# LayerNorm statistics of x rows 4 to 7 moved to ScalarE, the filter's constant term in 32-column quarters, four PSUM buffers for part of the products, 22 warm-up matmuls, new instruction orders

## The chip, the cores and the metric

One core of one Trainium2 chip. The time is device time of one execution in microseconds (us); the profile gives one execution in detail. Engines: TensorE (PE, its weight loads PEld), VectorE (DVE), ScalarE (ACT), GpSimd (POOL), and SyncE (SP), which issues most of the DMAs.

## The reference, cut to what matters

The kernel computes the output and the nine gradients of one transformer-like block. `mod` is silu(c) times a weight matrix, cut into six rows; part A is a spectral filter, part B a two-layer MLP with squared ReLU. x has 2048 rows of 512 in bf16, the MLP is 1792 wide.

```python
mod = (silu(c) @ w_mod).reshape(6, -1)
sa, ca, ga, sb, cb, gb = mod
h = layernorm(x) * (1 + ca) + sa
x = x + ga * irfft2(rfft2(h) * (w_r + 1j * w_i))
h = layernorm(x) * (1 + cb) + sb
r = max(einsum('bsd,df->bsf', h, w1) + b1, 0)
x = x + gb * (einsum('bsf,fd->bsd', r * r, w2) + b2)
```

Returned are x and, for a given gradient of it, the gradients of all inputs.

## The kernel before, in words

x is held as 16 row tiles of 128 rows by 512 columns (t = 0 to 15; "rows 4 to 7" are tiles of that numbering). The Fourier transforms are matmuls with cosine and sine tables that the kernel computes itself. The MLP's width is cut into 14 chunks of 128 columns, the 2048 rows into 4 blocks of 512 (b = 0 to 3).

The work around the change, in the order of the code:

- **Start.** A loop of 30 matmuls of a constant (L759 and L760, operand ones_sq) writes the two PSUM buffers mm_0s and mm_1s of pool mmps; nothing reads the results. silu(c) is spread over 128 columns by four ACT copies (L768) into scb, a part of the tile that the profile calls gab. `build_ta` (L124 to L128) makes a sine table. SP loads x in four pieces of 512 KB (L727), w2 in three (L735), w_mod in pieces (L724), the first block of the output's gradient (L742).
- **mod.** `mod_rows(1)` multiplies w_mod with scb (L784) and ACT writes 1 + ca to modb (L785). `mod_rows(2, 5, 4, 3)` computes four rows at once in 32-column strips of the array (L789).
- **Turned operands.** `turn_w2` turns w2 by TensorE (L814), and DVE or ACT (L817, L819) writes it to w2T, through PSUM pool psW with two buffers; `turn_g0` does the same for the first gradient block (L825; DVE L827, ACT L829) into gT_0s.
- **LayerNorm and first transform.** `row_stats` takes two row tiles: one bn_stats each (L837) and bn_aggr (L838) on DVE, then the reciprocal standard deviation and nb, minus the mean times it (L842). `row_norm` normalises (L847), stores (L849), multiplies by modb (L851), folds (`fold1`, L277 and L278); then four matmuls for each row tile (L313, L314) and an ACT eviction (L315) write utcs.
- **Products.** `back_products(b)`: for each chunk four matmuls of 512 columns (L912, w2T by gT) into a buffer of mmps, evicted into gab by DVE (L914, every fifth chunk) or ACT (L916). The products of blocks 0 to 2 are spread by the order table between the other work.
- **The constant term.** sa, the constant that LayerNorm's output gets, is transformed separately: 16 matmuls of 128 columns (L891), one DVE eviction (L892) to dcrow, and two matmuls (L350) with the 0/1 mask ind add it into the first second-stage tile psB.
- **Second stage.** `spec_f23`: matmuls into psB (L355), one ACT eviction to AE (L359), third-stage matmuls into psC (L338), ACT eviction (L339). ACT also makes tables lf_w for it from integer phases (L250).
- **Later.** The MLP forward and backward (L1086 to L1121, L1095 adds up a bias gradient), the weight gradients (L1389), the filter's backward pass, in which a helper copies PSUM to gmbc (ACT, L490), multiplies it four times on DVE (L500), and complex products p are made on DVE (L444, L445).

The order on every engine is not that of the code: the table `ORDER` (from L505) lists for PE, DVE, ACT, POOL and SP the numbers of all their instructions, and `set_order` chains each engine's instructions in that order. An engine executes its list strictly one after the other.

Of the kernel before, what the change touches and what calls it, by code (L numbers as in the profile page):

```python
# [9 lines left out]
AF = mybir.ActivationFunctionType  # L10
ALU = mybir.AluOpType
# [7 lines left out]
D = 512  # L19
# [305 lines left out]
def spec_f23(tc, K, UT, AEs, dc, dest, elementwise, after=lambda gi: None):  # L325

    nc = tc.nc
    with Slots(tc, name="psB", bufs=1, space=PSUM) as psB_pool, \
# [14 lines left out]
        for gi in range(8):  # L343
            ps = psB_pool.tile([P, 2, 2, 256], FP32, name="psB")
            for hh in range(2):
                for b in (1, 0):
                    extra = dc is not None and gi == 0 and hh == 0 and b == 0
                    if extra:
                        for cs in range(2):
                            nc.tensor.matmul(ps[64 * cs:64 * cs + 64, hh, b, :], lhsT=dc[0], rhs=dc[1][:, 256 * cs:256 * cs + 256], start=True, stop=False,  # L350
                                             tile_position=(0, 64 * cs))
                    for e in range(2):
                        for cs in range(2):
                            c = 2 * e + cs
                            nc.tensor.matmul(ps[64 * cs:64 * cs + 64, hh, b, P * e:P * e + P], lhsT=UT[:, c, 2 * (2 * gi + hh) + b, :, :],  # L355
                                             rhs=K["Cd"][:, P * c:P * c + P], start=not extra, stop=(e == 1 if extra else True), tile_position=(0, 64 * cs))
# [113 lines left out]
class GMod:  # L470
# [12 lines left out]
    def emit(self, jc, q, row, pool, ppool, nbuf=2, last=False):  # L483
# [147 lines left out]
def kernel(  # L631
# [286 lines left out]
    for b in range(NB - 1):  # L918
        back_products(b)
# [744 lines left out]
```

## Time and profile before

| | |
|---|---|
| median of 3 runs | 390.41 us (390.37 to 390.8) |
| profiled execution | 391.62 us |
| its span (first to last instruction) | 389.8 us, so 1.82 us lie around it |
| PE busy | 376.9 us, 97% |
| DVE busy | 336.1 us, 86% |
| ACT busy | 303.9 us, 78% |
| POOL busy | 35.1 us, 9% |
| granted TensorE clock, mean of the span | 1.00 |

How to read it: busy time is an average over stages that differ. The stages used here are cut at events that the trace shows: the first product (14.80 us), the first psB matmul (46.86), the first psG matmul of the transform back (70.51), and the end of that transform near 99.75. A timeline row gives start and duration in us, engine, source line, operation, out<-in, shape, count, and in brackets how long the engine stood idle before and which instruction released it.

### The profile page before, as it was taken

Reading aid. Unit: us, or ns where it says so; the run is one execution under the profiler, and the core shown is the slowest. Engines: PE = TensorE matmul, PEld = TensorE weight load, DVE = VectorE, ACT = ScalarE, POOL = GpSimd, SP = SyncE. Lnnn points to the kernel's source line nnn. Section 1 sums busy time; section 2 is a strip of 40 time slices with the busy share of each in tenths; the row PEclk is TensorE's granted clock in tenths of the full one; section 3 lists DMA queues with packets and bytes.
Section 4 is the critical chain, followed back from the end, with each engine's and each line's share of the span. In section 5 each row is a group of like instructions: output and inputs, shape, how many; then the busy total and the mean of one; then the engine's idle time right before and its main releaser. Section 6 shows DMA issues by size and latency. Waiting matters only on the chain. (4 is left out here: it accounts for less than half of the span.)

```text
span 389.8 us, 8395 instructions
## 1 busy us (share of the span) xinstructions
PE 376.9 (97%) x3027; PEld 205.1 (53%) x3051; DVE 336.1 (86%) x823; ACT 303.9 (78%) x601; POOL 35.1 (9%) x117
## 2 busy tenths in 40 slices
PE   7999999989999999999999999999899999999996
PEld 2565677544444444444444445447678655444455
DVE  5999969959897479999999999992999976989975
ACT  4787999889888489859986998347476458889793
POOL 5652011000000000000000000010022000010111
DMA  8997989954696869559938899999899989999997
GB/s 273 366 250 201 227 157 229 307 177 176 202 241 154 215 163 183 124 122 281 305 77 176 204 265 190 284 266 314 216 273 321 257 216 298 207 288 223 255 297 231
DMA packets 132429, 89.75 MB, mean 230 GB/s; under 512 B 86974, under 2 KB 118212, under 8 KB 132132
## 3 DMA queue, kind: packets, MB, share of 16 engines
q1 hardware_dynamic: 131376, 86.79, 87.5%
q0 software_dynamic: 832, 2.36, 1.7%
q8 instruction: 24, 0.39, 0.4%
q14 instruction: 17, 0.14, 0.1%
q10 hardware_dynamic: 180, 0.07, 0.1%
HBM read 39.23 MB, written 31.36 MB: 181 GB/s over the span
## 5 line engine op out<-in xcount | busy, mean ns | idle before, releaser
L1389 PEld LDWEIGHTS <-h_sb 128*64 128x64 bf16 (+1 forms) x464 | 32.3, 109 | 14.7 <-issue 2.1
L1086 PEld LDWEIGHTS <-w 128*128 128x128 bf16 x224 | 21.3, 98 | 27.0 <-issue 3.0
L1389 PE MATMUL mm_0s<-gab,h_sb 128*64 128x384 bf16 (+2 forms) x288 | 35.0, 345 | 0.2 <-DMA h_sb<-h_dram 0.2
L1095 ACT ACTIVATE gab<-gab 128x512 bf16<-128x512 bf16 x56 | 34.8, 629 | 0.0
L1121 PEld LDWEIGHTS <-gab 128*128 128x128 bf16 x224 | 21.7, 98 | 24.7 <-ACT gab L1095 0.3
L912 PEld LDWEIGHTS <-w2T 128*128 128x128 bf16 (+1 forms) x280 | 24.2, 102 | 18.3 <-issue 3.8
L1488 PEld LDWEIGHTS <-gab 128*128 128x128 bf16 x192 | 18.6, 98 | 17.8 <-issue 1.4
L1121 PE MATMUL og_1s<-w1T,gab 128*128 128x512 bf16 x111 | 26.9, 379 | 0.1
L1121 PE MATMUL og_0s<-w1T,gab 128*128 128x512 bf16 x106 | 26.5, 379 | 0.2
L1389 PE MATMUL mm_1s<-gab,h_sb 128*64 128x512 bf16 (+2 forms) x176 | 23.7, 370 | 1.4 <-ACT gmbc L490 1.4
L1086 PE MATMUL mm_1s<-h2T,w 128*128 128x512 bf16 x84 | 23.2, 379 | 0.8 <-ACT gab L916 0.3
L1086 PE MATMUL mm_0s<-h2T,w 128*128 128x512 bf16 x80 | 21.9, 379 | 0.0
L1488 PE MATMUL mm_1s<-g_sb,gab 128*128 128x512 bf16 (+1 forms) x95 | 19.7, 352 | 0.4 <-DVE g_sb L1510 0.4
L1488 PE MATMUL mm_0s<-g_sb,gab 128*128 128x512 bf16 (+1 forms) x93 | 19.8, 352 | 0.1
L359 ACT ACTIVATE AE<-psB 128x1024 bf16<-128x1024 f32 x16 | 16.6, 1039 | 1.4 <-issue 1.2
L912 PE MATMUL mm_0s<-gT_0s,w2T 128*64 128x512 bf16 (+1 forms) x76 | 16.6, 380 | 0.6 <-DVE gab L914 0.5
L1086 PE MATMUL pst<-h2T,w 128*128 128x512 bf16 x60 | 16.9, 379 | 0.0
L912 PE MATMUL mm_0s<-gT_1s,w2T 128*128 128x512 bf16 (+1 forms) x64 | 16.0, 379 | 0.3
L912 PE MATMUL mm_1s<-gT_1s,w2T 128*128 128x512 bf16 (+1 forms) x68 | 16.1, 379 | 0.2
L912 PE MATMUL mm_1s<-gT_0s,w2T 128*128 128x512 bf16 (+1 forms) x72 | 15.8, 379 | 0.0
L321 POOL MEMSET AE<- 128x4 bf16 x4 | 0.5, 116 | 167.7 <-DVE h_6s L1089 167.7
L916 ACT CAST gab<-mm_1s 128x512 bf16<-128x512 f32 x24 | 14.3, 597 | 1.4 <-PE mm_1s L912 1.2
(619 smaller groups left out, 1045.3 us busy)
## 6 DMA issues: line engine op xcount, KB each, us to landing
w<-in_B_w_dram SPq DMA_DIRECT2D x2, 1792.0 KB, 7.1
Xb<-xs_dram SPq DMA_DIRECT2D x4, 514.0 KB, 6.2
Z<-wz_dram SPq DMA_DIRECT2D x4, 514.0 KB, 6.3
x_sb<-in_A_x_dram SPq DMA_DIRECT2D x4, 512.0 KB, 7.2
n_dram<-x_sb SPq DMA_DIRECT2D x4, 512.0 KB
h_dram<-h2r SPq DMA_DIRECT2D x8, 256.0 KB, 2.8
gx_dram<-n2rows SPq DMA_DIRECT2D x8, 256.0 KB, 5.1
h_sb<-h_dram SPq DMA_DIRECT2D x4, 512.0 KB, 4.7
```

Of the source, the lines that this page charges most:

```text
L321: nc.gpsimd.memset(ae[:, :, :, 256:257], 0.0)
L359: nc.scalar.activation(dst, ps.rearrange("p r b (e f) -> p (r b) f e", e=2), AF.Copy, scale=EF_S)
L912: nc.tensor.matmul(ps[m], lhsT=w2T[:, dc, fc * P + m.start:fc * P + m.stop], rhs=gT[b][:, :, dc, :], start=(dc == 0), stop=(dc == 3), **pos)
L916: nc.scalar.copy(out=gaT[b][:, fc, :], in_=ps)
L1086: nc.tensor.matmul(ps, lhsT=w1[:, dc, (fc + i) * P:(fc + i + 1) * P], rhs=h2T[b][:, :, dc, :], start=(dc == 0), stop=(dc == 3))
L1095: nc.scalar.activation(gh[:, i, :], gh[:, i, :], AF.Copy, accum_out=gb1[:, b, fc + i:fc + i + 1])
L1121: nc.tensor.matmul(ps, lhsT=lhs(fc), rhs=rhs[:, fc, :], start=(fc == 0), stop=(fc == NFC - 1))
L1389: nc.tensor.matmul(blocks(ps[m], fb), lhsT=h2_sb[:, t, dc * P + m.start:dc * P + m.stop], rhs=gh_rows(t, fb), start=(t == 0), stop=(t == N ...
L1488: nc.tensor.matmul(ps[:, 0:w], lhsT=h_rows(fc, t), rhs=g_sb[:, t, c:c + w], start=(t == 0), stop=(t == NT - 1))
```

## The change

Six edits, and new tables for all five engines' orders:

1. Statistics of row tiles 4 to 7 (`row_stats_act`): ACT sums each row tile with a Copy that accumulates, and sums the squared deviations with a Square that accumulates; three small POOL operations and the same reciprocal replace bn_stats and bn_aggr of these four tiles.
2. The constant term in quarters: its four parts lie in four 32-partition strips, so 16 matmuls of a 32-column operand at four places of the array (four side by side) replace 16 of a 128-column one; the eviction has 128 instead of 512 columns, and the two matmuls that add it become four of half the width. The masks are written by POOL instead of DVE.
3. w2's and the gradient's PSUM tiles in psW get the shape of a product's tile, and products 9 to 13 of block 0 and 0 to 9 of block 1 go round over four buffers (two of mmps, two of psW) instead of two.
4. 22 instead of 30 matmuls of the constant at the start.
5. One ACT copy of 512 columns instead of four of 128 for scb.
6. New orders on every engine.

```diff
@@ spec_f23
-                    if extra:
-                        for cs in range(2):
-                            nc.tensor.matmul(ps[64 * cs:64 * cs + 64, hh, b, :], lhsT=dc[0], rhs=dc[1][:, 256 * cs:256 * cs + 256], start=True, stop=False, ...
+                            if extra:
+                                nc.tensor.matmul(ps[64 * cs:64 * cs + 64, hh, b, P * e:P * e + P], lhsT=dc[0][:, c], rhs=dc[1], start=True, stop=False, ...
@@ ORDER (five tables, all numbers new; first line of PE's)
-        "0 2 1 4 3 6 5 8 30 10 7 12 9 14 11 16 13 18 15 31 52 56 53 57-58 17 54 20 55 19 59 32-47 21-25 64-67 60-63 27 26 29 "
+        "1 0 3 5 7 9 22 11 2 4 13 6 8 15 44 10 23 48-51 17 12 24-39 45-47 14 16 18 52-59 19-21 68-74 60 75 61-67 40-43 238-242 "
@@ main
-    nc.vector.memset(ind, 0.0)
-    nc.vector.memset(ind[0:1, :, 0:1], 1.0)
+    nc.gpsimd.memset(ind, 0.0)
+    for k in range(4):
+        nc.gpsimd.memset(ind[32 * k:32 * k + 32, k, :, 0:1], 1.0 / 32)
-    for k in range(30):
+    for k in range(22):
-    for dc in range(4):
-        nc.scalar.activation(scb[:, dc, :], ccolf[:, dc:dc + 1].broadcast_to([P, P]), AF.Copy, scale=sigcol[:, dc:dc + 1])
+    nc.scalar.copy(out=scb, in_=sc[:, :, None].broadcast_to([P, 4, P]))
@@ turn_w2 (turn_g0 likewise)
-        ps = psW.tile([P, 8, P], BF16, name="psW")
+        ps = psW.tile([P, D], FP32, name="psW").bitcast(BF16).rearrange("p (a q) -> p a q", a=8)
@@
+    def row_stats_act(t):
+        dev = p0.tile([P, 2], FP32, name="l1_dev", bufs=4)
+        nm = p0.tile([P, 2], FP32, name="l1_nm", bufs=4)
+        for j in range(2):
+            junk = p0.tile([P, D], BF16, name="l1_junk", bufs=2)
+            nc.scalar.activation(junk, x_sb[:, t + j, :], AF.Copy, accum_out=dev[:, j:j + 1])
+        nc.gpsimd.tensor_scalar(nm, dev, -1.0 / D, None, op0=ALU.mult)
+        for j in range(2):
+            junk = p0.tile([P, D], BF16, name="l1_junk", bufs=2)
+            nc.scalar.activation(junk, x_sb[:, t + j, :], AF.Square, bias=nm[:, j:j + 1], accum_out=dev[:, j:j + 1])
+        i1 = inv1[:, t:t + 2]
+        nc.gpsimd.tensor_scalar(dev, dev, 1.0 / D, None, op0=ALU.mult)
+        rstd(nc, i1, dev, K)
+        nbs[t] = p0.tile([P, 2], FP32, name="l1_nb", bufs=4)
+        nc.gpsimd.tensor_tensor(nbs[t], nm, i1, op=ALU.mult)
+
     def row_stats(t):
+        if t in (4, 6):
+            return row_stats_act(t)
@@
-    for c, neg in enumerate(((), (1, 3), (1, 2), (2, 3))):
-        fs, co = slice(P * c, P * c + P), (0, 2, 1, 3)[c]
-        for i in range(4):
-            k = int(i in neg)
-            nc.tensor.matmul(psd[:, P * co:P * co + P], lhsT=sacol[:, k, i:i + 1].broadcast_to([P, P]), rhs=K["Cd"][:, fs], start=(i == 0), stop=(i == 3))
+    for i in range(4):
+        for k, neg in enumerate(((), (1, 3), (1, 2), (2, 3))):
+            nc.tensor.matmul(psd[32 * k:32 * k + 32, :], lhsT=sacol[:, int(i in neg), i:i + 1].broadcast_to([P, 32]), rhs=K["Cd"][:, P * k:P * k + P],
+                             start=(i == 0), stop=(i == 3), tile_position=(0, 32 * k))
@@ back_products
-    def back_products(b):
+    def back_products(b, wide=()):
         for fc in range(NFC):
-            ps = mmps.tile([P, SB], FP32, name="mm")
+            k = (fc in wide and wide.index(fc)) % 4
+            ps = psW.tile([P, D], FP32, name="psW") if k > 1 else mmps.tile([P, SB], FP32, name="mm")
...
-    for b in range(NB - 1):
-        back_products(b)
+    back_products(0, range(9, NFC))
+    back_products(1, range(10))
+    psW.release()
+    psM.release()
+    psF1.release()
+    back_products(2)
```

**ACT ahead of modb.** ACT's list before the first product, before the change (L785 writes modb, L819 and L829 write the first products' operands w2T and gT_0s):

```order
L768 ACTIVATE gab<-ccolf,sigcol 128x128
L819 ACTIVATE w2T<-psW_0s,gb2x 128x512
L829 COPY gT_0s<-psW_1s 128x1024
L785 ACTIVATE modb<-mod_ps,onef 128x512
L916 CAST gab<-mm_1s 128x512
```

and the same place of the changed kernel (its L839 and L843 are the sums and squared sums, L786 writes modb, L830 gT_0s):

```order
L839 ACTIVATE l_junk_0s,l_dev_1s<-x_sb 128x512
L839 ACTIVATE l_junk_1s,l_dev_1s<-x_sb 128x512
L820 ACTIVATE w2T<-psW_0s,gb2x 128x512
L769 COPY gab<-sacol 128x512
L830 COPY gT_0s<-psW_1s 128x1024
L843 ACTIVATE l_junk_1s,l_dev_1s<-x_sb,l_nm_1s 128x512
L843 ACTIVATE l_junk_0s,l_dev_1s<-x_sb,l_nm_1s 128x512
L786 ACTIVATE modb<-mod_ps,onef 128x512
L820 ACTIVATE w2T<-psW_0s,gb2x 128x640
```

All eight new activations stand ahead of modb, two of them between gT_0s and modb; the other four stand earlier in the list.

**ACT at the first AE.** Before (L359 evicts psB, L250 makes a table):

```order
L178 ACTIVATE Cf<-gen_v_1s,npi 128x512
L916 CAST gab<-mm_0s 128x512
L359 ACTIVATE AE_123<-psB 128x4x256
L250 ACTIVATE lf_w_1s<-lf_v,npi 128x1024
L916 CAST gab<-mm_1s 128x512
L359 ACTIVATE AE_124<-psB 128x4x256
```

and after (L358 evicts psB, L931 a product):

```order
L315 CAST utcs<-psA_0s 128x128x4
L250 ACTIVATE lf_w_1s<-lf_v,npi 128x1024
L358 ACTIVATE AE_123<-psB 128x4x256
L931 CAST gab<-psW_1s 128x512
```

The fourth table L250 has moved from behind the first AE to ahead of it, and products now sit in psW as well.

**DVE in the backward filter.** Before (L500 reads gmbc, L444 and L445 make complex products, all on DVE):

```order
L500 SCALAR_TENSOR_TENSOR gm_junk,gsc<-wmc_0s,onef,gmbc 128x512
L445 TENSOR_TENSOR p_3967<-Xb,G_0s 128x1028
L444 TENSOR_TENSOR p_3966<-Xb,G_0s 128x1028
L500 SCALAR_TENSOR_TENSOR gm_junk,gsc<-wmc_0s,onef,gmbc 128x512
L446 TENSOR_TENSOR Xb<-p_3966 128x2x257
```

and after:

```order
L499 SCALAR_TENSOR_TENSOR gm_junk,gsc<-wmc_0s,onef,gmbc 128x512 x2
L445 TENSOR_TENSOR Z_3880<-p_3956 128x2x257
L444 TENSOR_TENSOR p_3963<-Xb,G_0s 128x1028
L499 SCALAR_TENSOR_TENSOR gm_junk,gsc<-wmc_0s,onef,gmbc 128x512
L443 TENSOR_TENSOR p_3962<-Xb,G_0s 128x1028
```

One product p instead of two stands between the third and the fourth of a group of four multiplications by gmbc.

On SP the third piece of x is now loaded fourth in all, ahead of the gradient's first block and the piece of w_mod that modb needs.

## Rows read from the trace of the kernel before

**Rows 1.** Windows by stage: us, busy PE PEld DVE ACT POOL, PEclk, DMA, GB/s.

```profile
0.00:14.80 14.80, 12.62 (x83) 5.85 (x85) 10.85 (x57) 6.70 (x12) 7.90 (x44) 1.00 0.90 305
14.80:46.90 32.10, 31.34 (x244) 18.42 (x245) 32.10 (x118) 27.81 (x47) 11.33 (x34) 1.00 0.92 246
46.90:70.50 23.60, 23.27 (x324) 17.35 (x323) 19.86 (x51) 23.36 (x39) 2.92 (x8) 1.00 0.97 203
...
250.00:389.80 139.80, 133.48 (x1308) 80.67 (x1313) 116.56 (x269) 97.95 (x185) 12.83 (x30) 1.00 1.02 263
```

**Rows 2.** Timeline of PE from the start to the first product.

```profile
2.54 0.63 PE L760 MATMUL mm_0s<-ones_sq 128*128 128x512 bf16 x1
2.97 0.63 PE L760 MATMUL mm_1s<-ones_sq 128*128 128x512 bf16 x1
...
6.89 0.38 PE L760 MATMUL mm_0s<-ones_sq 128*128 128x512 bf16 x1
...
13.72 1.03 PE L784 MATMUL mod_ps<-wm_0s,gab 128*128 128x512 bf16 x3
...
14.80 1.03 PE L912 MATMUL mm_1s<-gT_0s,w2T 128*128 128x512 bf16 x4
```

**Rows 3.** Timeline of ACT, 4 to 15 us.

```profile
8.43 0.40 ACT L124 ACTIVATE TA<-ta_v,npi 128x128 bf16<-128x128 int32 x1 [1.93 <-DVE ta_v L121]
8.74 0.97 ACT L768 ACTIVATE gab<-ccolf,sigcol 128x128 bf16<-128x128 f32 x3
11.05 0.69 ACT L819 ACTIVATE w2T<-psW_0s,gb2x 128x512 bf16<-128x512 bf16 x1 [1.34 <-DVE gb2x L807]
...
13.59 1.01 ACT L829 COPY gT_0s<-psW_1s 128x1024 bf16<-128x1024 bf16 x1 [0.54 <-PE psW_1s L825]
14.79 0.69 ACT L785 ACTIVATE modb<-mod_ps,onef 128x512 bf16<-128x512 f32 x1 [0.19 <-PE mod_ps L784]
```

**Rows 4.** Timeline of SP's queue, and DMA issues to 20 us with time to landing.

```profile
1.67 0.43 SPq L735 DMA_DIRECT2D gab<-in_B_w_dram  x1
...
gab<-in_B_w_dram SPq DMA_DIRECT2D x1, 512.0 KB, 6.4
```

**Rows 5.** Windows: 10 to 20 us.

```profile
10.00:20.00 10.00, 9.77 (x93) 5.84 (x93) 9.96 (x38) 7.50 (x12) 6.33 (x27) 1.00 1.08 365
```

**Rows 6.** Line L837 on DVE, one buffer: ns min/median/max, first and last start.

```profile
L837 DVE BATCH_NORM_STATS2 l_st_1s<-x_sb x4: 675/680/695, 5.1 to 32.3; 128x6 f32<-128x512 bf16 x4
```

**Rows 7.** Groups of ACT instructions that accumulate: busy us, mean ns.

```profile
L1095 ACT ACTIVATE gab<-gab 128x512 bf16<-128x512 bf16 x56 | 34.8, 629 | 0.0
L1095 ACT ACTIVATION_READ_ACCUMULATOR gab<-gab 128x1 f32 x56 | 11.2, 200 | 0.0
```

**Rows 8.** Timeline of PE: four-strip matmuls, a waiting product, the constant term.

```profile
29.97 0.60 PE L789 MATMUL mod_ps<-wm_1s,gab 128*32 128x512 bf16 x2
...
31.55 0.38 PE L912 MATMUL mm_0s<-gT_0s,w2T 128*128 128x512 bf16 x1 [0.54 <-DVE gab L914]
...
41.48 0.89 PE L891 MATMUL mod_ps<-Cd,sacol 128*128 128x128 bf16 x13
42.20 1.03 PE L912 MATMUL mm_0s<-gT_1s,w2T 128*128 128x512 bf16 x4
```

**Rows 9.** Timeline of DVE: the last fold ahead of the second stage.

```profile
44.61 0.41 DVE L278 TENSOR_TENSOR fold_u_1s<-h_1s 128x512 bf16<-128x512 bf16 x1
```

**Rows 10.** Timeline of ACT: the table behind the first AE.

```profile
48.63 1.14 ACT L250 ACTIVATE lf_w_1s<-lf_v,npi 128x1024 bf16<-128x1024 int16 x1
```

**Rows 11.** Timelines of DVE, ACT and PE around 276 us.

```profile
275.91 0.69 DVE L444 TENSOR_TENSOR p<-Xb,G_0s 128x1028 bf16<-128x1028 bf16 x1
276.51 0.74 DVE L500 SCALAR_TENSOR_TENSOR gm_junk<-wmc_0s,onef,gmbc 128x512 bf16<-128x512 bf16 x1
...
277.37 0.59 ACT L490 CAST gmbc<-mm_1s 128x512 bf16<-128x512 f32 x1 [2.65 <-DVE gm_junk L500]
...
278.01 1.70 PE L1389 MATMUL mm_1s<-gab,h_sb 128*64 128x512 bf16 x14 [1.37 <-ACT gmbc L490]
```

More of the change, by code (lines that the diff above doesn't have):

```diff
@@ L347, in spec_f23 @@
                     extra = dc is not None and gi == 0 and hh == 0 and b == 0
-                    if extra:
-                        for cs in range(2):
-                            nc.tensor.matmul(ps[64 * cs:64 * cs + 64, hh, b, :], lhsT=dc[0], rhs=dc[1][:, 256 * cs:256 * cs + 256], start=True, stop=False,
-                                             tile_position=(0, 64 * cs))
                     for e in range(2):
@@ L354, in spec_f23 @@
                             c = 2 * e + cs
+                            if extra:
+                                nc.tensor.matmul(ps[64 * cs:64 * cs + 64, hh, b, P * e:P * e + P], lhsT=dc[0][:, c], rhs=dc[1], start=True, stop=False,
+                                                 tile_position=(0, 64 * cs))
                             nc.tensor.matmul(ps[64 * cs:64 * cs + 64, hh, b, P * e:P * e + P], lhsT=UT[:, c, 2 * (2 * gi + hh) + b, :, :],
-                                             rhs=K["Cd"][:, P * c:P * c + P], start=not extra, stop=(e == 1 if extra else True), tile_position=(0, 64 * cs))
+                                             rhs=K["Cd"][:, P * c:P * c + P], start=not extra, stop=True, tile_position=(0, 64 * cs))
             ae = AEs[gi % 2]
@@ L681 @@
     AEs = make_ae(nc, lfp)
-    dcrow = lfp.tile([P, D], BF16, name="dcrow")
-    ind = lfp.tile([P, NT, 4], BF16, name="ind")
-    nc.vector.memset(ind, 0.0)
-    nc.vector.memset(ind[0:1, :, 0:1], 1.0)
+    dcrow = lfp.tile([P, P], BF16, name="dcrow")
+    ind = lfp.tile([P, 4, NT, 4], BF16, name="ind")
+    nc.gpsimd.memset(ind, 0.0)
+    for k in range(4):
+        nc.gpsimd.memset(ind[32 * k:32 * k + 32, k, :, 0:1], 1.0 / 32)
     gen = Slots(tc, name="gen", bufs=1, side="right")
@@ L821, in turn_g0 @@
     def turn_g0(h):
-        ps = psW.tile([P, 2, 4, P], BF16, name="psW")
+        ps = psW.tile([P, D], FP32, name="psW").bitcast(BF16).rearrange("p (j c q) -> p j c q", j=2, c=4)
         for j in range(2):
@@ L885 @@
     pm = K["pm"]
-    psd = psM.tile([P, D], FP32, name="mod_ps", bufs=1)
-    for c, neg in enumerate(((), (1, 3), (1, 2), (2, 3))):
-        fs, co = slice(P * c, P * c + P), (0, 2, 1, 3)[c]
-        for i in range(4):
-            k = int(i in neg)
-            nc.tensor.matmul(psd[:, P * co:P * co + P], lhsT=sacol[:, k, i:i + 1].broadcast_to([P, P]), rhs=K["Cd"][:, fs], start=(i == 0), stop=(i == 3))
+    psd = psM.tile([P, D], FP32, name="mod_ps", bufs=1)[:, 0:P]
+    for i in range(4):
+        for k, neg in enumerate(((), (1, 3), (1, 2), (2, 3))):
+            nc.tensor.matmul(psd[32 * k:32 * k + 32, :], lhsT=sacol[:, int(i in neg), i:i + 1].broadcast_to([P, 32]), rhs=K["Cd"][:, P * k:P * k + P],
+                             start=(i == 0), stop=(i == 3), tile_position=(0, 32 * k))
     nc.vector.tensor_scalar(dcrow, psd, 128.0, None, op0=ALU.mult)
@@ L901 @@
         nc.sync.dma_start(LF_dram[q], K["LFall"][:, q])
-    psW.release()
-    psM.release()
-    psF1.release()
-    def back_products(b):
+    def back_products(b, wide=()):
         for fc in range(NFC):
-            ps = mmps.tile([P, SB], FP32, name="mm")
+            k = (fc in wide and wide.index(fc)) % 4
+            ps = psW.tile([P, D], FP32, name="psW") if k > 1 else mmps.tile([P, SB], FP32, name="mm")
             for dc in range(4):
@@ L947, in ew_f @@
                 back_products(NB - 1)
-        spec_f23(tc, K, UT, AEs, (ind.rearrange("p a b -> p (a b)"), dcrow), dest_f, ew_f)
+        spec_f23(tc, K, UT, AEs, (ind.rearrange("p c a b -> p c (a b)"), dcrow), dest_f, ew_f)
     lfp.release()
```

182 rows, old and new, of the table ORDER are left out of this document.

## The prediction

> **What bounds the kernel now.** I read the windows by stage first, to see which engine is full where, and then the timelines at the borders of the stages.
>
> Up to 14.80 us no engine is full: DVE is busy for 10.85 us, ACT for 6.70, and PE's 12.62 are mostly matmuls of the constant [rows 1]. What ends this stage is the first product, which needs w2T and gT_0s; gT_0s comes from the copy at 13.59, which lasts 1.01 us, and the product starts at 14.80 [rows 2, 3]. So the start is set by loads, turned operands and their evictions.
>
> From 14.80 to 46.90 DVE is busy in all of 32.10 us, PE in 31.34 and ACT in 27.81 [rows 1]. The stage ends when the last fold, at 44.61 [rows 9], has gone through its matmuls and ACT's eviction. From 46.90 to 70.50 ACT is busy in 23.36 of 23.60 us and PE in 23.27 [rows 1]. In both stages PE is almost full, because products fill its gaps: the idle time of PE is 0.76 and 0.33 us. That is the ceiling for anything that only relieves DVE or ACT there; more can be had only by taking work from PE. From 250 us on PE is idle for 6.32 us [rows 1], and one wait there stands in the way of a single move of the order: 1.37 us at 278.01, for gmbc [rows 11].
>
> **The change part by part.** The sum is made against the profiled execution, 391.62 us, of which 389.8 are span; the median of the runs is 390.41, which is 1.21 lower, and I carry the sum over to it. A measurement of this kernel can tell about 0.2%, 0.78 us, from no change.
>
> *Eight matmuls of the constant fewer.* At the pace of products, four in 1.03 us of which the last shows 0.38, one takes (1.03 - 0.38) / 3 = 0.216 us, so eight are 1.73 us [rows 2]. They fill time in which PE waits for turned operands. Bounds -1.73 and 0; I take 0, since the first product follows ACT's copy and not the matmul before it.
>
> *Loads.* x's third piece is moved ahead of the gradient and of w_mod. 512 KB at the 365 GB/s of 10 to 20 us [rows 5] are 1.44 us. w2's first piece lands at 1.67 + 6.4 = 8.07 us [rows 4]; two more pieces of 512 KB behind it put the gradient at 10.9 and w_mod's at 12.4 now, and at 12.4 and 13.8 after the change. The matmuls on w_mod's piece start at 13.72 now [rows 2], so about 0.1 is lost; bounds 0 and +1.44. With the eviction behind it I take **+0.15** for the first product.
>
> *Statistics.* Four bn_stats of 0.68 us leave DVE [rows 6], -2.7 us of its work. ACT gets eight activations, each with the read of its accumulator: 0.63 us when the 0.20 of the read overlaps, 0.83 when it doesn't [rows 7], in the middle 0.73, 5.8 us in all (5.0 to 6.6). One copy for scb instead of four gives back about 0.7: three took 0.97, so four 1.29, and a 512-column activation takes 0.59 to 0.69 [rows 3, 11]. The 5.1 us left go ahead of modb. ACT's waits there are 1.93, 1.34, 0.54 and 0.19, together 4.0 [rows 3]. So modb comes about 1.1 us later, and behind it in ACT's list stand w2T's evictions; DVE's first multiplication by modb waits for it, and of the 2.7 us some 1.6 are left. PE's ceiling then cuts it: without more idle time on PE the last fold's earlier end is worth what the next two terms say, and nothing by itself. Bounds: 0, and -0.76 if all of PE's idle time goes.
>
> *Four buffers.* The longest wait of a product is 0.54 us, at 31.55, for DVE to evict mm_0s [rows 8]; a product with two more buffers doesn't wait. **-0.5** (bounds -0.76, 0). Covered is it by DVE's order; a later DVE eviction can bring it back.
>
> *The constant in quarters.* Between 41.48 and 42.20 thirteen matmuls of 128 columns pass, 0.055 each [rows 8], 16 take 0.89. In strips of 32 columns two of the same strip start 0.216 apart while the other strips run beside them (two in 0.60 at 29.97) [rows 8], so four strips cost one: 4 x 0.055 = 0.22. **-0.67**; the other bound is 0, if strips of 128 columns don't overlap. The two matmuls into psB become four of half the columns: 0. The shorter eviction and the masks on POOL free DVE a little, under the same ceiling: 0.
>
> Here a rule speaks against the edit. The row shows four-strip matmuls next to full ones without a wait named before or after them [rows 8]. The Trainium skill, page TensorEngine Tiling (Array Packing), section Key Properties, says that a change of the tiling mode drains TensorE; by it the strips would pay for going in and out of the mode, and if that cost all they save, the sum would be -1.3 and the time 389.1. I stay with the row, which is the same kind of matmul in the same place.
>
> *The table behind the first AE.* The 1.14 us of L250 [rows 10] leave the stage in which ACT is full, and go into one in which it has 4.29 us idle [rows 1]. PE can use no more than its 0.33: **-0.3** (bounds -0.33, 0).
>
> *The late wait.* One product p of 0.60 us (275.91 to 276.51) less stands ahead of the multiplication that frees gmbc [rows 11]; PE's wait of 1.37 falls to about 0.7: **-0.65** (bounds -1.37, 0). Late next would be ACT's copy of 0.59 itself.
>
> *Other orders.* Every engine's list is new. The rest keeps the same stages, so 0, with 1 us on each side.
>
> Sum: 0.15 - 0.5 - 0.67 - 0.3 - 0.65 = -1.97, from 391.62 to 389.65 and from the median to **388.4 us**.
>
> **The rivals.**
>
> *The start pays too.* If the matmuls of the constant now hold up the turned operands in PE's list, eight fewer bring the first product forward by up to 1.73: 388.4 - 1.7 = 386.7. For it: PE is busy in 12.62 of 14.80 us. Against: ACT's copy is what the product follows, and its loads move back. Chance 0.10.
>
> *Nothing of DVE's time is used.* modb comes as late as DVE has been relieved, the strips don't overlap, and only the late wait is shorter, -0.5 to -0.65: about 389.9, within the bound. For it: three engines are nearly full in one stage, and what one gives another takes. Chance 0.18.
>
> *Slower: ScalarE becomes the bound.* At 0.83 us each the activations take 6.6 us, of which 4.3 fit (the 4.0 of the waits and a third of a microsecond at the copies): modb and all behind it come 2.3 us late. From 14.80 to 46.90 ACT then has 27.81 + 1.14 + 2.3 = 31.25 of 32.10 us, as tight as PE is now, and with PE's and DVE's results arriving in between it gets nothing back; the first AE comes 2.3 late: 390.41 + 2.3 - 0.65 = 392.1. It decides once modb's delay passes the 2.7 us that DVE saves less what DVE can do in the meantime, or ACT's idle time in this stage falls below about 1 us. Against: DVE has the normalisation of other rows to do until modb is there. By the rows, two activations of 0.63 to 0.83 replace 0.68 of DVE [rows 6, 7], 1.9 to 2.4 times the engine time per row tile. Chance 0.12. The Trainium skill, ScalarE: Activation LUTs, section Rules for kernel authors, has a rule on this side: simple arithmetic belongs on VectorE, which it gives as up to about three times faster per element in bf16. The rows agree in direction.
>
> *Slower: the clock.* The granted clock is at its lower level first: at 2.54 the matmuls are 0.43 us apart, while at 14.80 they are 0.216 apart, so 1.2 and 2.4 GHz [rows 2]. With fewer matmuls of the constant PE does less ahead of the first product. Of the 12.62 us that PE is busy there [rows 1], the 30 matmuls of the constant, about 12 at the lower level and 18 at the higher in that timeline, take 12 x 0.43 + 18 x 0.216 = 9.0, so needed work is 3.6; if the clock stays low until the first product, that takes up to 3.6 longer: 388.4 + 3.6 = 392.0. Against: 22 remain, and the rise comes before 6.89, where a matmul already shows 0.38 instead of 0.63 [rows 2]. Chance 0.05. The Trainium skill, TensorE: Matmul & The Clock Gate, Part 1, states that the throttled level is the default and that activity lifts it; the trace agrees.
>
> **How the numbers follow.** The forecast has the remaining 0.55, with 387.2 to 389.6 as its own range (the terms at their bounds partly add and partly cancel). Faster: forecast and first rival, 0.65. Same: 0.18. Slower: the two last, 0.17. The range from 385.9 to 391.2 holds the forecast, the start's full gain with some luck in the orders, and all of no change, and leaves out most of the slower cases.
>
> **What would show it.** In the changed profile: first product between 14.5 and 15.3; modb's eviction ending near 16.6; DVE no longer full from 14.8 to 46.9; no product of blocks 0 and 1 waiting for an eviction; the 16 strip matmuls in 0.2 to 0.3 us; first AE about 1 us earlier; PE's wait near 276 us at about 0.7. Wrong it is if the first AE comes later than now, if ACT is full ahead of it, or if new waits of over 1 us stand on PE behind 70 us, where I put the new orders at nothing.

## The result and the profile after

The changed kernel takes 394.44 us (median of 4, 393.78 to 394.82) beside 390.39 for the kernel before on the same chip: 1.0107 times as long, 95% interval 1.0081 to 1.0132. It is slower by 4 us where 388.4 was forecast, and outside the range. A second series on another chip gave 394.92 beside 389.74, ratio 1.0115 (1.0085 to 1.0145). The profiled execution took 394.82 us with a span of 393.1.

The windows by stage of the changed kernel, with the columns of [rows 1], cut at the same events (first product, first psB, first psG, end of that transform, first weight-gradient matmul, a little behind the column sums that follow):

```profile
0.00:14.53 14.53, 12.96 (x75) 5.29 (x77) 9.17 (x48) 9.93 (x21) 7.63 (x41) 1.00 0.88 301
14.53:45.80 31.27, 30.80 (x242) 17.37 (x241) 31.17 (x116) 28.92 (x51) 12.21 (x47) 1.00 1.02 262
45.80:68.95 23.15, 22.81 (x326) 16.52 (x325) 18.79 (x48) 22.88 (x38) 2.95 (x9) 1.00 0.98 221
68.95:96.30 27.35, 26.70 (x324) 14.52 (x325) 20.18 (x45) 25.14 (x49) 0.00 (x0) 1.00 0.87 242
96.30:254.90 158.60, 156.17 (x799) 71.46 (x812) 143.85 (x306) 127.05 (x282) 0.00 (x0) 1.00 0.81 188
254.90:266.00 11.10, 7.97 (x58) 3.07 (x56) 5.17 (x11) 1.66 (x3) 1.30 (x6) 0.69 0.93 275
266.00:393.10 127.10, 120.21 (x1208) 75.97 (x1212) 103.96 (x243) 91.03 (x172) 13.32 (x26) 1.00 0.96 256
```

The three last stages of the kernel before, by the same events:

```profile
99.75:256.70 156.95, 155.19 (x788) 71.16 (x800) 140.27 (x298) 125.73 (x279) 0.12 (x1) 1.00 0.84 201
256.70:262.20 5.50, 5.27 (x58) 2.42 (x56) 5.40 (x11) 2.12 (x5) 0.67 (x3) 1.00 1.12 329
262.20:389.80 127.60, 121.56 (x1215) 74.92 (x1218) 104.50 (x243) 91.85 (x174) 12.17 (x28) 1.00 1.00 261
```

Against [rows 1] each of the first three stages is shorter, by 0.27, 0.83 and 0.45 us, and the fourth too (27.35 instead of 29.25). At 96.3 us the changed kernel is ahead by 3.4. It then loses 1.65 in the MLP, and 5.6 in one stretch: 58 matmuls that took 5.50 us take 11.10, at a mean granted clock of 0.69. That stretch on TensorE:

```profile
254.97 1.05 PE L1408 MATMUL mm_0s<-gab,h_sb 128*64 128x512 bf16 x8
259.16 5.33 PE L1408 MATMUL mm_0s<-gab,h_sb 128*64 128x512 bf16 x24 [3.13 <-DMA h_sb<-h_dram]
```

and SP's queue ahead of it (start, issue time, what is loaded):

```profile
246.50 0.58 SPq L1283 DMA_DIRECT2D h_sb<-h_dram  x1
247.18 1.23 SPq L1090 DMA_TRANSPOSE gab<-gab  x1
248.45 2.30 SPq L1276 DMA_TRANSPOSE hr<-h_6s  x1
250.79 2.23 SPq L1276 DMA_TRANSPOSE hr<-h_2s  x1
253.07 1.07 SPq L1283 DMA_DIRECT2D h_sb<-h_dram  x2
```

The first weight gradient reads h_sb in four quarters of 512 KB. The new order issues two of them only from 253.07 on, behind two transposing loads of hr, which is first read at 333.8, about 80 us later. TensorE is through with the first quarter at 256.0 and waits until 259.16. The kernel before, in the same place:

```profile
253.75 0.87 SPq L1264 DMA_DIRECT2D h_sb<-h_dram  x1
...
256.72 1.92 PE L1389 MATMUL mm_0s<-gab,h_sb 128*64 128x512 bf16 x16
258.87 1.92 PE L1389 MATMUL mm_0s<-gab,h_sb 128*64 128x512 bf16 x16 [0.23 <-DMA h_sb<-h_dram]
```

There too the last quarter was issued late, at 253.75, but TensorE had 16 matmuls to do before it and waited 0.23. In SP's table the four loads are 172 to 175, in the order in which TensorE reads them. Before they stood as 175 173 172 174, now as 172 175 174 173: the last to be issued, at 253.7 in both kernels, was the third to be read and is now the second, wanted after 8 matmuls. And the changed kernel begins the gradient 1.75 us earlier. Of the 2.9 us by which its wait is longer, the rows add up to 1.75 for the earlier start, 0.9 for the order and 0.3 for the later landing (259.16 instead of 258.87).

The granted clock (the third last column) follows, in windows of 1 us:

```profile
257.00:258.00 1.00, 0.00 (x0) 0.00 (x0) 0.97 (x2) 0.00 (x0) 0.00 (x0) 1.00 1.01 344
258.00:259.00 1.00, 0.00 (x0) 0.00 (x0) 1.00 (x3) 0.00 (x0) 0.00 (x0) 0.57 0.93 342
259.00:260.00 1.00, 0.84 (x4) 0.36 (x6) 0.91 (x3) 0.00 (x0) 0.00 (x0) 0.50 1.10 363
...
264.00:265.00 1.00, 1.00 (x12) 0.29 (x12) 0.00 (x0) 0.47 (x1) 0.00 (x0) 0.51 0.03 6
265.00:266.00 1.00, 1.00 (x23) 0.46 (x12) 0.23 (x1) 0.12 (x1) 0.00 (x0) 1.00 1.12 212
```

TensorE has done nothing since 256.0; by 259 the clock is at its lower level, 1.2 GHz (0.50), and it stays there until 265, with TensorE busy from 259.16 on. The Trainium skill, TensorE: Matmul & The Clock Gate, Part 1, calls the throttled level the default that activity lifts; the rows agree, with 1.00 again from 265.

### The profile page after: what moved, and what is told of

It is laid out like the page before. It is cut to its first block, busy times and chain, and to the rows that moved or that the text cites. A ratio compares the mean times of both kernels' runs of the same rounds, so it can differ in the third digit from the quotient of the medians.

```text
span 393.1 us, 8396 instructions
## 1 busy us (share of the span) xinstructions
PE 377.6 (96%) x3021; PEld 204.2 (52%) x3045; DVE 332.3 (85%) x811; ACT 306.6 (78%) x614; POOL 37.4 (10%) x128
## 4 chain that ended last, share of the span: by engine, by line
PE 49%; DVE 20%; DMA 11%; ACT 11%; SPq 5%; issue 3%; DVEq 0%; ACTq 0%
PE og_0s L1140 8%; PE og_1s L1140 7%; PE mm_0s L1408 7%; PE mm_1s L1408 4%; PE mm_0s L1507 4%; PE mm_1s L1507 4%; DMA g_sb<-in_grad_out_dram 3%; SPq L1276 2%; PE mm_0s L1105 2%; PE mm_1s L1105 2%; DMA gab<-in_B_w_dram 2%; PE mm_1s L927 2%; DMA Z<-in_A_w_r_dram 2%; DMA x_1s<-in_A_x_dram 1%; DMA h_sb<-h_dram 1%
## 5 line engine op out<-in xcount | busy, mean ns | idle before, releaser
L1408 PEld LDWEIGHTS <-h_sb 128*64 128x64 bf16 (+1 forms) x464 | 34.7, 112 | 15.8 <-DMA h_sb<-h_dram 3.6
L1408 PE MATMUL mm_0s<-gab,h_sb 128*64 128x384 bf16 (+2 forms) x288 | 36.3, 365 | 3.1 <-DMA h_sb<-h_dram 3.1
L927 PEld LDWEIGHTS <-w2T 128*128 128x128 bf16 (+1 forms) x280 | 23.2, 102 | 17.7 <-issue 2.9
L1140 PE MATMUL og_0s<-w1T,gab 128*128 128x512 bf16 x108 | 27.4, 379 | 0.5 <-ACT gab L1114 0.2
L358 ACT ACTIVATE AE<-psB 128x1024 bf16<-128x1024 f32 x16 | 16.6, 1040 | 3.6 <-PE psB L354 2.8
L400 PEld LDWEIGHTS <-utcs 128*128 128x128 bf16 x128 | 10.3, 98 | 9.1 <-issue 1.5
L927 PE MATMUL mm_1s<-gT_0s,w2T 128*128 128x512 bf16 (+1 forms) x68 | 14.6, 380 | 0.0
L927 PE MATMUL mm_1s<-gT_1s,w2T 128*128 128x512 bf16 (+1 forms) x60 | 14.3, 378 | 0.1
L927 PE MATMUL mm_0s<-gT_0s,w2T 128*64 128x512 bf16 (+1 forms) x72 | 14.2, 379 | 0.0
L927 PE MATMUL mm_0s<-gT_1s,w2T 128*128 128x512 bf16 (+1 forms) x56 | 14.1, 378 | 0.0
## 6 DMA issues: line engine op xcount, KB each, us to landing
h_dram<-h2r SPq DMA_DIRECT2D x8, 256.0 KB, 4.7
gx_dram<-n2rows SPq DMA_DIRECT2D x8, 256.0 KB, 4.9
```

Source lines behind the costliest of these rows:

```text
L358: nc.scalar.activation(dst, ps.rearrange("p r b (e f) -> p (r b) f e", e=2), AF.Copy, scale=EF_S)
L400: nc.tensor.matmul(ps[:, P * i:P * i + P], lhsT=CS[:, i, t].rearrange("p a b -> p (a b)"), rhs=K["Cf"][:, i, :], start=True, stop=True)
L927: nc.tensor.matmul(ps[m], lhsT=w2T[:, dc, fc * P + m.start:fc * P + m.stop], rhs=gT[b][:, :, dc, :], start=(dc == 0), stop=(dc == 3), **pos)
L1140: nc.tensor.matmul(ps, lhsT=lhs(fc), rhs=rhs[:, fc, :], start=(fc == 0), stop=(fc == NFC - 1))
L1408: nc.tensor.matmul(blocks(ps[m], fb), lhsT=h2_sb[:, t, dc * P + m.start:dc * P + m.stop], rhs=gh_rows(t, fb), start=(t == 0), stop=(t == N ...
```

## The experiments

Each run is compared by its ratio to the kernel before on the same chip, since chips differ by more than some of the effects (389.68 to 390.39 us for the kernel before); the 95% interval stands in brackets. 1% is 3.9 us.

**The two loads moved up.** One move in SP's table (174 and 173 are the two quarters, 170 and 161 the transposing loads):

```diff
-"... 166 175 178 170 161 174 173 162 154 ..."
+"... 166 175 178 174 173 170 161-162 154 ..."
```

> The changed kernel with one move in SP's order: the two loads of h2_sb (a quarter each, 512 KB) that are issued at 253.07 and 253.69 us go ahead of the two transposing loads of hr at 248.45 and 250.79. Theory A, the loss is this late load and the clock that falls while TensorE waits for it: the wait of 3.13 us at 259 is gone, the granted clock of the whole run is back at 1.00, the stretch from the first weight-gradient matmul to the column sums takes about 5.5 us instead of 11.1, and the time is about 389 us (388 to 390.5). Theory B, the new late orders are tight in many places and the next wait takes its place, such as the transposes that now come later: 392.5 to 394.5 us.

It took 391.75 us, ratio 1.0052 (1.0028 to 1.0075), with a clock of 0.999. And on another chip:

> The changed kernel with the two h2_sb loads moved up once more, for the same chip: 1.5 us above the kernel before (0.9 to 2.2).

It took 392.96 us, ratio 1.0081 (1.0067 to 1.0094), 3.2 above the kernel before and outside the 0.9 to 2.2 expected. Against the changed kernel's 1.0107 and 1.0115 the move gives back 0.55% and 0.34% (2.1 and 1.3 us): a part, as neither theory had it. The profile of the first of the two shows why. The stretch is nearly cured: the last column sum starts at 260.1 instead of 265.3. The load that is waited for is issued 4.8 us earlier but lands only 2.4 us earlier, so that a short wait is left:

```profile
256.73 2.78 PE L1320 MATMUL mm_0s<-gab,h_sb 128*64 128x512 bf16 x24 [0.76 <-DMA h_sb<-h_dram]
```

And TensorE's next waits come up (engine, tile, line, what ended it: us in total, times, longest):

```profile
PE mm_1s L487 <- POOL sel L1241: 1.1, 1, 1.1
PE mm_1s L1320 <- ACT gmbc L489: 1.0, 1, 1.0
PE psY_1s L410 <- ACT Tsb_1s L402: 1.0, 1, 1.0
...
PE mm_0s L1320 <- DMA h_sb<-h_dram: 0.8, 1, 0.8
PE mm_0s L1419 <- DVE g_sb L1441: 0.5, 1, 0.5
```

The first of them, for a mask that GpSimd writes, was not in the changed kernel's list of waits: there TensorE came 5 us later. Not tried was the smaller edit, an exchange of 175 and 173 alone, which keeps the transposing loads in their place.

**The wait filled.** TensorE's idle time gets work, and the load stays late. The 14 matmuls stand in TensorE's list just ahead of the one that waits; the single one, ahead of the gradient, keeps the two buffers in turn:

```diff
+    fps = mmps.tile([P, 4, P], FP32, name="mm")
+    nc.tensor.matmul(fps, lhsT=K["ones_sq"], rhs=K["ones_sq"][:, None, :].broadcast_to([P, 4, P]), start=True, stop=True)
+    fps = mmps.tile([P, 4, P], FP32, name="mm")
+    for k in range(14):
+        nc.tensor.matmul(fps, lhsT=K["ones_sq"], rhs=K["ones_sq"][:, None, :].broadcast_to([P, 4, P]), start=True, stop=True)
```

> The changed kernel with 14 matmuls of the constant put into TensorE's list just ahead of the matmul that waits for h2_sb (and one more of them ahead of the first weight gradient, to keep the buffers' turn). Only the wait's idle time is filled, the load is as late as before. Theory A, the wait of 3.1 us also makes the granted clock fall, and that costs as much again: the clock stays at 1.00, the stretch from the first weight-gradient matmul to the column sums takes about 8.4 us instead of 11.1 (5.5 of the kernel before plus the wait), and the time is 391.7 us (391 to 392.7). Theory B, the lower clock there costs nothing by itself, since the next loads are late as well: 394 to 395 us.

It took 391.79 us, ratio 1.0060 (1.0041 to 1.0079), with a clock of 1.00: theory A in the clock and in the stretch, and 1.8 us (2.1 against the second series) by the ratios where 2.7 were expected. TensorE in this kernel:

```profile
255.12 1.05 PE L1320 MATMUL mm_0s<-gab,h_sb 128*64 128x512 bf16 x8
256.11 3.20 PE L1348 MATMUL mm_1s<-ones_sq 128*128 128x512 bf16 x14
259.24 2.78 PE L1320 MATMUL mm_0s<-gab,h_sb 128*64 128x512 bf16 x24
```

The load lands at the same time, near 259.2. Behind the wait 24 matmuls take 5.33 us in the changed kernel and 2.78 here, and the last column sum starts at 262.6 instead of 265.3. So in the stretch the clock that fell during the wait costs 2.7 us, nearly as much as the wait; about 2 of them reach the end.

**Seams between the two orders.** Four kernels take one kernel's order for all that starts before a time and the other's for the rest, on all five engines; of each table SP's numbers at the seam stand here.

```diff
 seam 96.3, changed program
-"... 60 71 61 62 125 66 68 69 ..."
+"... 60 71 121 68 62 66 63 69 ..."
 seam 99.7, program before, changed rest
-"... 60 59 62 66 65 63 73 69 ..."
+"... 60 59 99 95 97 65 73 71 ..."
 seam 130, changed program
-"... 120 79 109 70 130 85 110 121 ..."
+"... 120 79 121 67 64 85 70 78 ..."
 seam 237, changed program
-"... 176 123 157 155 177 164 172 159 ..."
+"... 176 123 170 166 164 159 168 175 ..."
```

> The changed kernel, its own orders for all that starts before 237 us, the orders of the kernel before behind. Theory A, ahead of 237 us the changed kernel keeps some 1.75 us of its 3.4, the rest having been lost in the MLP's new orders (158.6 us instead of 156.95), and only the late orders cost: 388.6 us (388.0 to 389.5), 1.6 above the kernel that goes over at 96.3. Theory B, the MLP's new orders cost nothing by themselves: the same as that kernel within 0.5.

It took 388.89 us, ratio 0.9970 (0.9943 to 0.9998): theory A in the time, and the first version that beats the kernel before, though narrowly. (That the kernel with the seam at 96.3 would be 1.6 us faster still did not come true, as shown below.) With the front and the start of the gradient as in the changed kernel, the old order again issues one quarter late, and TensorE has 16 matmuls to do before it:

```profile
252.92 0.43 SPq L1195 DMA_DIRECT2D h_sb<-h_dram  x1
...
254.86 1.92 PE L1320 MATMUL mm_0s<-gab,h_sb 128*64 128x512 bf16 x16
257.05 1.92 PE L1320 MATMUL mm_0s<-gab,h_sb 128*64 128x512 bf16 x16 [0.27 <-DMA h_sb<-h_dram]
```

The repeat:

> The kernel with the changed orders up to 237 us and the old ones behind once more, for its interval on the chip on which the changed kernel runs too. 1.36 us under the kernel before (1.0 to 1.8).

It took 388.70 us, ratio 0.9973 (0.9952 to 0.9995), 1.04 us under the kernel before. The changed kernel ran beside it:

> The changed kernel once more beside the others: 4 us above the kernel before (3.2 to 4.8), granted clock of the profiled run 0.99, the wait for h2_sb 3.1 us (2.5 to 3.7).

It took 394.92 us, ratio 1.0115, with a clock of 0.991; its wait for h_sb was 3.8 us and the time 5.2 above, both a little over the ranges expected. So with the same front the new late orders cost 394.92 - 388.70 = 6.2 us on this chip; from the first runs it is 4.05 + 1.36 = 5.4 us.

> The kernel before with its orders up to 99.7 us and the changed kernel's orders behind. Theory A, gains and losses add: the rest costs 4.05 + 3.4 = 7.4 us, so about 397.8 us (396 to 399), with the wait for h2_sb and a granted clock below 0.8 around 260 us. Theory B, the rest's loss hangs on arriving early there (a load that lands at a time of its own is waited for only by an engine that is ahead): the wait is shorter by what the front is late, 392 to 394.5 us.

It took 396.47 us, ratio 1.0175 (1.0139 to 1.0210), 6.2 over the kernel before, with a wait for h_sb of 3.7 us and the clock at 0.84 from 257.3 to 268.2. That is theory A, at the low end: the old front makes it no better. TensorE reached the gradient at 257.3, 2.4 us later than in the changed kernel, and waited longer still: the two loads are issued from 255.91 on, 2.8 us later, with the rest of SP's list. So the lead alone doesn't make the wait.

> The changed kernel, its own orders for all that starts before 96.3 us (the end of the first filter), and from there on the orders of the kernel before on all five engines. Theory A, the front is worth the 3.4 us by which the changed kernel is ahead there, and the old rest keeps it: 387.0 us (386.3 to 387.9), no wait of over 1 us for h2_sb. Theory B, the 3.4 us are only work moved behind the border or idle time that comes back as waits for the loads of the MLP's weights: 389 to 390.5 us.

It took 391.12 us, ratio 1.0030 (0.9997 to 1.0062): a miss, nearer to theory B. Behind the seam TensorE waits, as its timeline shows,

```profile
99.83 0.38 PE L1017 MATMUL mm_1s<-h2T,w 128*128 128x512 bf16 x1 [1.45 <-DVE h2T L992]
100.43 0.38 PE L1017 MATMUL mm_1s<-h2T,w 128*128 128x512 bf16 x1 [0.22 <-ACT h2T L994]
```

and the lead over the kernel before is down to 0.6 us where the MLP's second layer begins (first matmul at 111.49 against 112.13). Part of the 3.4 us is work put behind the border. The first 13 us of the MLP, before and after:

```profile
99.75:112.10 12.35, 12.00 (x61) 5.49 (x59) 11.40 (x23) 10.57 (x20) 0.00 (x0) 1.00 0.99 267
```

```profile
96.30:109.90 13.60, 13.24 (x66) 6.14 (x66) 13.10 (x29) 11.45 (x23) 0.00 (x0) 1.00 0.91 233
```

TensorE has 66 matmuls there instead of 61 and is busy for 1.24 us more, so 1.2 of the 3.4 was never won; some 2.2 were, and 0.4 more go until 255 (145.00 us instead of 144.60).

> The changed kernel, its own orders for all that starts before 130 us, the orders of the kernel before behind: the seam lies inside the MLP, where both lists are in step. Theory A, the new orders of the MLP cost 1.65 us by themselves (158.6 instead of 156.95) and the old ones don't: 387.4 us (386.8 to 388.2), 1 to 1.5 below the kernel with the seam at 237. Theory B, the lead at 96 us is partly idle time that is paid back in the MLP's first matmuls in whichever order: 388.4 to 389.6.

It took 389.26 us, ratio 0.9998 (0.9966 to 1.0030): theory B. With the old orders the MLP takes 159.5 us from 96.35 to the first weight gradient, no less than with the new ones (158.6).

**The statistics back on VectorE**, in the best kernel (seam at 237):

```diff
-        if t in (4, 6):
-            return row_stats_act(t)
-        mv = p0.tile([P, 2, 2], FP32, name="l1_mv", bufs=4)
+        mv = p0.tile([P, 2, 2], FP32, name="l1_mv", bufs=8)
-            st = p0.tile([P, 6], FP32, name="l1_st", bufs=4)
+            st = p0.tile([P, 6], FP32, name="l1_st", bufs=8)
```

with the four bn_stats early in VectorE's list, ahead of the copy of gT_0s:

> The kernel with the changed orders up to 237 us and the old ones behind, with the statistics of rows 4 to 7 back on VectorE (four bn_stats with their bn_aggr early in its list, two buffers' worth more for the small results, ScalarE's eight activations and six small GpSimd operations gone). Theory A, TensorE is the ceiling there and the move by itself is worth little: the first second-stage matmul within 0.3 us of 45.9, the time 388.9 us within 0.6. Theory B, VectorE's 2.7 us were the bound of the stage: the first second-stage matmul 1 to 2.7 us later, 390 to 391.5 us.

It took 392.49 us, ratio 1.0058 (1.0033 to 1.0083), more than theory B. The first product waits for VectorE's copy of gT_0s and comes at 17.43 instead of 14.6:

```profile
17.43 0.82 PE L837 MATMUL mm_0s<-gT_0s,w2T 128*128 128x512 bf16 x3 [1.59 <-DVE gT_0s L740]
```

From there to psB the stage takes 31.67 us, 0.4 more than with the change, VectorE having done the four bn_stats before. And behind that copy (the same code; 41 to 44 and 51 to 54 are the bn_stats and bn_aggr in VectorE's table, 25 is the copy):

```diff
-"... 27 29 41-44 177 32 ... 64 34 51-54 71 73 25 72 30 ... 36 184 120 37 168 46 ..."
+"... 27 29 177 32 ... 64 34 71 73 25 41-44 72 30 ... 36 184 120 37 51-54 168 46 ..."
```

> As the kernel with the statistics of rows 4 to 7 back on VectorE, but with the four bn_stats behind the copy of gT_0s in VectorE's list, so that the first product is not behind them. Theory A, VectorE is still full from the first product on in the changed orders (busy in 31.17 of 31.27 us), so its 2.7 us of work come back as a later last fold: the first product stays at 14.6 (within 0.3), the first second-stage matmul comes 1 to 2.7 us later than 45.9, the time 389.8 to 391.5 us. Theory B, TensorE was the ceiling: within 0.4 of 45.9 and 388.9 us.

It took 393.57 us, ratio 1.0115 (1.0076 to 1.0155), more than theory A. The first product stays at 14.55; then TensorE waits for VectorE's eviction of a product:

```profile
20.03 1.02 PE L837 MATMUL mm_0s<-gT_0s,w2T 128*128 128x512 bf16 x4 [3.04 <-DVE gab L839]
```

The clock falls with it (0.95 from 14.6 to 46), and psB starts at 50.65, 4.7 us late. Beside the best kernel's 0.9973 the two places cost 0.85% and 1.42% (3.3 and 5.5 us; the medians of the second and of the best kernel, on one chip, are 4.9 apart). Both put the bn_stats ahead of something that TensorE waits for, in lists that were made without them, so this is the price of these two places, and the move by itself may be worth less. A third place in VectorE's list might cost less; that wasn't tried, and neither was the move alone on the kernel before.

**Single edits on the kernel before.** Fewer matmuls of the constant, the eight ahead of the first product taken out:

```diff
-    for k in range(30):
+    for k in range(22):
```

> The kernel before with one edit: 22 instead of 30 matmuls of the constant, the eight nearest to the first product taken out of TensorE's list. Theory A, they only fill time in which TensorE waits for turned operands: the first product within 0.25 us of 14.8, the same time as the kernel before within 0.5 us, clock 1.00 throughout. Theory B, they hold up the turned operands: the first product up to 1.7 us earlier, 388.7 us. Theory C, they keep the clock up: the clock falls ahead of the first product and the time is 1 to 3 us longer.

It took 391.02 us, ratio 1.0025 (0.9997 to 1.0052), with the first product at 14.93 and a clock of 0.999: theory A, as far as the interval tells, and nothing for B or C. And four buffers:

```diff
-    for b in range(NB - 1):
-        back_products(b)
+    back_products(0, range(9, NFC))
+    back_products(1, range(10))
+    psW.release()
+    psM.release()
+    psF1.release()
+    back_products(2)
```

(with the tiles of psW and `back_products` as in the change)

> The kernel before with its own orders and one edit: products 9 to 13 of block 0 and 0 to 9 of block 1 go round over four PSUM buffers instead of two. Theory A, the wait of 0.54 us at 31.55 is gone and the first second-stage matmul comes 0 to 0.6 us earlier; 389.9 us, not to be told from no change. Theory B, the order table was laid for two buffers, and an evicting engine that is full makes the same product wait elsewhere: no change of either.

It took 390.32 us, ratio 1.0010 (0.9992 to 1.0027). The wait of [rows 8] is gone, and the stage is as long as before, as this window from first product to psB shows:

```profile
14.91:46.97 32.06, 31.47 (x243) 18.15 (x242) 32.06 (x118) 27.85 (x47) 11.33 (x34) 1.00 0.95 249
```

VectorE is still busy all the time. Theory B.

**Where the rest of the late loss lies.** The kernel with the two loads moved, with seams at 262.5 and at 326.8:

```diff
 seam 262.5
-"... 180 183 181 185 187 186 218 182 ..."
+"... 180 183 196 185 187 186 188 190 ..."
 seam 326.8
-"... 224 253 245 261 236 251 256 252 ..."
+"... 224 253 252 243 236 255 256 244 ..."
```

> The changed kernel with the two h2_sb loads moved up, its orders for all that starts before 262.5 us (behind the column sums), the orders of the kernel before behind. Theory A, the 2.9 us that still lie between the kernel with the two loads moved and the one with all old orders from 237 us on are lost behind 262.5, in the backward filter and the last weight gradients: 388.8 us (388.2 to 389.6). Theory B, they are lost between 237 and 262.5: 391 to 392.

It took 390.47 us, ratio 1.0024 (1.0001 to 1.0048): between the two theories.

> The same with the seam at 326.8 us, at the first matmul of the last weight gradient. Theory A, the last 60 us hold most of the 2.9 (59.0 us against 57.1 from the first of these matmuls to the last): 389.7 us (389.2 to 390.3). Theory B, the backward filter holds it (a wait of 1.07 us for sel at 262.9, among others): 391 to 392.

It took 392.37 us, ratio 1.0067 (1.0052 to 1.0082). With 392.96 for no seam on this chip, some 0.6 us are lost behind 327, within the noise of the two intervals, and 1.9 between 262.5 and 327. Theory A of the second run falls, and B holds, a little beyond its figure. From the kernel with the seam at 262.5, 0.24% over the kernel before, to the one with the seam at 237, 0.3% under it, it is another 0.5%, or 2 us. But the seam at 262.5 makes a wait of its own, 2.0 us for gmbc (1.0 without a seam), and behind it the clock is at 0.50 again, so that 24 matmuls that take 2.78 us without a seam take 4.47:

```profile
277.01 4.47 PE L1320 MATMUL mm_1s<-gab,h_sb 128*64 128x512 bf16 x24 [2.01 <-ACT gmbc L489]
```

Wait and clock are 2.7 us in their stretch, so the 2 us can be the seam's, and it is not shown that the orders between 237 and 262.5 still cost anything with the two loads moved. What is left of the loss goes with several waits of around 1 us (sel, gmbc, Tsb, g_sb), none of which was taken away alone: that they are its cause is not shown.

## Why the prediction was wrong

*The step that failed* is the last term, "Other orders": "Every engine's list is new. The rest keeps the same stages, so 0, with 1 us on each side." The late orders cost 5.4 to 6.2 us. I compared the stages' order on TensorE and did not follow SP's list behind 100 us, in which two quarters of h_sb had got behind two transposing loads, the one read second as the last. SP's list could be read before any run; one has to ask of every load whether it now stands behind something that is needed later. The load and the clock behind it are the part of the loss that is shown: moving the two loads gave back 1.3 to 2.1 us. Some 3 to 4 us remain against the kernel with old orders from 237 us on (1.0052 and 1.0081 beside 0.9970 and 0.9973), and their cause stays open, beyond the new waits of about 1 us. The prediction did name the sign, waits of over 1 us on TensorE behind 70 us: two came, 3.1 us for h_sb and 1.4 for g_sb.

*The wait's price.* Even a step that had seen the load would have had to count the clock. The wait of 3.13 us cost 5.6 in its stretch, and the filled wait shows that 2.7 of it are the clock. The clock fell in a place where no rival had put it: behind the longest wait. At the start 22 matmuls are as good as 30. There the column of the granted clock reads 1.00, and the spacing of the matmuls shows the lower level, 0.43 us as in the prediction; it lasts until about 9 us in the changed kernel and 6.3 before, and the first product is no later.

*The front, -1.32 without the late wait.* The kernel with the old orders from 237 us on is 1.04 and 1.36 us faster. That the sum fits is luck. The front's lead includes some 0.7 us won in the fourth stage, for which there was no term (1.9, less the 1.24 of work put behind its border), and of the terms three were wrong in size or reason:

- *Four buffers, -0.5*: 0 alone. *Statistics, "nothing by itself"*: putting them back cost 3.3 to 5.5 us in two places of the changed lists. I had taken PE's 0.76 us of idle time for the ceiling and DVE for covered, with DVE busy in 32.10 of 32.10 [rows 1]. In the second of them the lateness of 4.7 us is a wait of 3.0 with the clock behind it. The stage became shorter by 0.83 with the change, and DVE's work in it by 0.93 (31.17 instead of 32.10). That fits VectorE as the bound, then and now (31.17 of 31.27), against what I wrote would show. It is argued and not shown alone, since PE's work in the stage shrank too, by 0.54.
- *The constant in quarters, -0.67.* The 16 matmuls run four side by side, in about 0.2 us, but they cost TensorE more than that, as these rows of the changed kernel show:

```profile
42.99 0.27 PE L313 MATMUL psA_0s<-TA,fold_u_0s 128*128 128x256 bf16 x1
43.10 0.27 PE L314 MATMUL psA_0s<-TA,fold_u_0s 128*128 128x256 bf16 x1
43.30 0.41 PE L908 MATMUL mod_ps<-Cd,sacol 128*32 128x128 bf16 x16
43.65 0.28 PE L313 MATMUL psA_1s<-TA,fold_u_1s 128*128 128x256 bf16 x1
```

At the pace of 0.11 the strips would start at 43.21; they start at 43.30, and the next full matmul at 43.65, about 0.1 us behind the end of their four rounds. So there is a pause of about 0.1 us at either change of form, the strips take 0.44 us instead of 0.89, and the term was worth 0.45 of TensorE's time. The rows before had the same pause without naming a wait: four matmuls of a product from 29.00 on, 0.216 apart, make room for the next at 29.86, and the first strip starts at 29.96. Whether the kernel's time got any of it is not shown, with VectorE as full as it is.

- *First product, +0.15*: 14.53 and 14.82 in two profiles, so -0.27 and 0; eight matmuls fewer, 0: right.
- *modb 1.1 us later*: right, at 0.9. Its eviction starts at 15.70 instead of 14.79, and each activation with its read costs 0.62 (the sums) to 0.71 (the squares), start to start:

```profile
11.07 0.62 ACT L839 ACTIVATE l_junk_0s<-x_sb 128x512 bf16<-128x512 bf16 x1
...
11.69 0.62 ACT L839 ACTIVATE l_junk_1s<-x_sb 128x512 bf16<-128x512 bf16 x1
...
15.00 0.72 ACT L843 ACTIVATE l_junk_0s<-x_sb,l_nm_1s 128x512 bf16<-128x512 bf16 x1
...
15.70 0.68 ACT L786 ACTIVATE modb<-mod_ps,onef 128x512 bf16<-128x512 f32 x1
```

- *The table behind the first AE, -0.3*: the stage is 0.45 shorter, with ACT busy for 22.88 us instead of 23.36; the move was not run alone.
- *The late wait, -0.65*: it is not among TensorE's waits in the changed kernel, but there TensorE is 5 us late; with the two loads moved it is 1.0 instead of 1.37, and the old orders behind 237 us show 0.8 as well. So -0.4 at most, and not by the order alone.

*The rivals.* ScalarE as the bound did not come: it is busy in 28.92 of 31.27 us and the first AE starts at 46.86 instead of 47.71. A row tile costs ScalarE 0.62 + 0.71 = 1.33 us and had cost VectorE 0.68, and still putting it back made the kernel slower, VectorE being the fuller engine. The Trainium skill, ScalarE: Activation LUTs, section Rules for kernel authors, puts simple arithmetic on VectorE: per instruction the rows agree, for this stage the two runs speak against it. That slower could come from a load out of place was no rival of mine, although "every engine's list is new" was the largest part of the diff.

## What to carry to other kernels

When a change brings new orders, compare the DMA queue's list over the whole program, not only the engines' around the edit: for each load, what it now stands behind, when that can issue, and when its reader comes. Price a wait on TensorE with the clock that may fall behind it: here 3.1 us cost 5.6 in their stretch, of which a part reached the end. And where one engine is busy in all of a stage, take its work for the bound even if another is at 98%: here a wait of TensorE that was taken away gave nothing as long as VectorE stayed full.

## What was not expected of the hardware

The clock's fall cost almost as much as the wait that led to it, and the lower level outlasted the wait by some 6 us (0.50 or 0.51 from 259 to 265) although TensorE was busy all that time. The clock fell again behind the wait of 2.0 us at 277 in the kernel with the seam at 262.5, and behind the one of 3.0 us at 20 us with the statistics back on VectorE. Matmuls that nobody reads, put into the wait, kept the clock at 1.00 and gave about as much (0.47% of the run's time) as moving the loads did (0.55% and 0.34%). Transposing loads held SP's queue for 1.2 to 1.3 us each between 239 and 244 us and for 2.2 to 2.3 us ahead of the late loads; behind the two loads moved up one held it for 5.4 us (251.15 to 256.59). So what stands behind them can be held up by more than their usual length.

A change between full-width and strip matmuls cost TensorE about 0.1 us each way, which no wait in the profile names.
